# GpSimd's stores become operations of the scheduler, with a price and places of their own

## The chip, the cores and the metric

The kernel runs on one NeuronCore of a Trainium2 chip. The metric is the device time of one execution in microseconds (us). Three runs of the kernel before gave 804.59, 804.32 and 807.07 us; their median is 804.59 us.

Engine names as the profile has them: PE is TensorE (matrix products), PEld its weight loads, DVE is VectorE, ACT is ScalarE, POOL is GpSimd, and SP is SyncE, which here only issues DMAs. An entry such as SPq or POOLq is the queue of DMA issues of that engine.

## The reference, cut to what matters

```python
def _A_ref(x, dft_seq_re, dft_seq_im, dft_hid_re, dft_hid_im):
    a = jnp.einsum("bsd,ed->bse", x, dft_hid_re)
    b = jnp.einsum("bsd,ed->bse", x, dft_hid_im)
    return jnp.einsum("ts,bse->bte", dft_seq_re, a) - jnp.einsum("ts,bse->bte", dft_seq_im, b)

def _B_ref(x, w_gate, w_up, w_down):
    g = jnp.einsum("bsd,df->bsf", x, w_gate)
    u = jnp.einsum("bsd,df->bsf", x, w_up)
    return jnp.einsum("bsf,fd->bsd", _gelu(g) * u, w_down)

xn = _layernorm(x, axis=-1)
return x + _A_ref(xn, ...) + _B_ref(xn, ...)
```

Here x is 1 x 2048 x 512, the sequence matrices are 2048 x 2048, the hidden ones 512 x 512, and the inner width of the gated part is 1792. All is float32. The change touches only how the first part, A, is put in order.

## The kernel before

**Products.** Each float32 operand is split into a high and a low part (ScalarE writes the high part at L241, VectorE the low part at L246), and a product is three matrix products on these parts. On top of that, most products use a scheme of seven block products in place of eight, so an r from 0 to 6 stands in many names.

**Stages.** Part A first multiplies with the sequence matrices: for each of four column blocks c of 512, panels of the matrices are loaded (tiles `pan`), added and subtracted on VectorE (L623, L624), split (`psh`, `psl`), and multiplied into the banks `m`. A step is one value k of this loop. In the first half of a block (p = 0) it loads three panels, makes four operands and runs 24 matrix products; one of its sums is also parked in DRAM (`t2_park`), for the second half (p = 1), which loads two panels and the parked one. After block 1 and block 3 the result is multiplied with the hidden matrices into the banks `y` (seven products r, in the order 0, 1 ahead of block 1 and 4, 2, 6, 5, 3 behind it). ScalarE copies each `y` bank to a tile `part`, and GpSimd stores that tile into the DRAM tensor `partial`. For r = 0, 5, 6 the store is plain; for r = 1, 2, 3, 4 it adds to what lies there (L544 and L546). Part B, the gated part, follows from about 387 us on and is not touched.

**Memory.** All working tiles come from one pool of 109 slots. A tile gets the slot of an older tile, and its first writer waits until the last reader of the older one is done. If that reader is a store, the writer waits until the store has landed.

**What sets the order.** From the start to the first steps of block 2, the order of every engine's instructions comes from a list scheduler, the class `Plan` (L31 to L208). Each operation has an engine, a cost in us, operations that it needs, tiles that it makes and uses, and sometimes a due date. `deadlines` works the other due dates out backwards from the products of TensorE. `run` then plays the program on a model of the five engines: at each turn `choose` takes, per engine, the operation that can start first, or one with an earlier due date that can start nearly as soon, and of these the one that starts first of all. The code of the operations is then emitted in that order, and so each engine's queue has it. The model has one DMA system, `self.dma`, which takes 2.6 us for a megabyte (L179), and a list of what is in flight (`flying`); SP may have eight loads in flight.

GpSimd's DMAs were entered in the model but not ordered by it: the store was issued inside another operation. The copy of `y` on ScalarE issued it (`y_out`, in the operation `yo`), the sum on VectorE issued the parked panel (`sum_step`) and the difference `xd` (`sub_xd`). An operation of GpSimd beside it (`yd`, `park`, `xdp`) did nothing but hold the model's GpSimd and DMA time:

```python
plan.add(("yo", r), "a", 1.04, lambda r=r: y_out(0, r), ...)
plan.add(("yd", r), "g", 1.2, lambda: None, after=[("yo", r)], uses=[("po", r)], mb=2 * MB)
```

From block 2 on, the order is written out by hand in loops; these call the same functions.

**Waits between engines.** SP's loads and GpSimd's stores each go through eight counters in rotation (DMAHW0 to 7, DMASW0 to 7). An issue waits until the DMA eight places before it has landed, since it uses the same counter; so a GpSimd row with `waits DMASW4` also raises DMASW4 itself.

Of the kernel before, what the change touches and what calls it, by code (L numbers as in the profile page):

```python
# [15 lines left out]
S = 2048  # L16
# [19 lines left out]
class Plan:  # L36
# [16 lines left out]
    def add(self, name, engine, cost, fn, after=(), makes=(), uses=(), due=None, mb=0, banks=(), holds=()):  # L53
# [5 lines left out]
        self.ops[name] = dict(e=engine, cost=cost, fn=fn, after=after, makes=dict(makes), due=due, mb=mb, banks=tuple(banks), drains=bool(holds) and engine != "p")  # L59
# [82 lines left out]
    def run(self):  # L142
# [25 lines left out]
        while any(ready.values()):  # L168
# [39 lines left out]
def fnet_geglu_kernel(ctx: ExitStack, tc: tile.TileContext, x, xt, cs, dh, wgu, wd, out):  # L208
# [300 lines left out]
    yps, zraw, zt = {}, {}, {}  # L509
# [14 lines left out]
    def sub_xd(sp, j):  # L524
        nc.vector.tensor_sub(xd[sp, j, 0], xd[sp, j, 0], xd[sp, j, 1])
        nc.gpsimd.dma_start(partial[sp, 2, j], xd[sp, j, 0])
# [11 lines left out]

    def y_out(sp, r, js=range(2)):
        for j in js:  # L540
            t = slot("part")
            nc.scalar.activation(t, yps[r, j], AF.Copy)  # L542
            if r in (0, 5, 6):
                nc.gpsimd.dma_start(partial[sp, r, j], t)  # L544
            else:
                nc.gpsimd.dma_start(partial[sp, r, j], t, accum_op=OP.add)  # L546
# [67 lines left out]
    def sum_step(i):  # L614
# [4 lines left out]
        if p == 0:  # L619
# [4 lines left out]
                    lambda: (nc.vector.tensor_sub(b22, b22, t1), nc.gpsimd.dma_start(t2_park[c, k], b22))]  # L624
# [610 lines left out]
    plan.flying["s"] = [4.4, 5.7, 7., 8.1]  # L1235
    for t in range(2, X_AHEAD):
        plan.done(("x", XO[t]), land)
        plan.flying["s"].append(land)
        land += .675
    for i in range(3, LOAD_AHEAD):  # L1240
        plan.done(("pan", i), land)
        plan.flying["s"].append(land)
# [145 lines left out]
    def step_ops(i, late=None):  # L1388
# [3 lines left out]
        def s(j):  # L1392
            if not box:
                box.extend(sum_step(i))
            box[j]()
        for key in (*PANELS[p], *(["t2"] if p else [])):
            plan.add(("ld", i, key), "s", .45, lambda key=key: load_one(i, key), makes={("r", i, key): 1}, mb=MB, due=late,
                     after=[("S", i - (HS - FIRST[c]), 2)] if key == "t2" else [])
        if p == 0:
# [5 lines left out]
            plan.add(("park", i), "g", .01, lambda: None, after=[("S", i, 2)], mb=MB, uses=[("r", i, b22)])  # L1405
# [169 lines left out]
    for r, g in ((0, 0), (0, 1), (1, 0), (1, 1)):  # L1575
# [3 lines left out]
        if g:  # L1579
            plan.add(("yo", r), "a", 1.04, lambda r=r: y_out(0, r), after=[("y", r, g), *([("res", 0, 0)] if r else ["st2"])],  # L1580
# [168 lines left out]
```

## Time and profile before

| what | before |
|---|---|
| median of three runs | 804.59 us |
| the profiled execution's own time | 804.45 us |
| its span, first to last instruction | 802.4 us |
| PE busy | 794.4 us (99%) |
| DVE busy | 718.8 us (90%) |
| ACT busy | 504.9 us (63%) |
| POOL busy | 156.4 us (19%) |
| granted clock of TensorE, mean over the core | 1.000 |
| stages on PE, from the chain of work that ended last: plain products / block 0 / y / block 1 | from 5.54 / 60.69 / 89.25 / 100.29 us |
| y again / block 2 / y / block 3 / y | from 176.28 / 205.12 / 283.77 / 294.65 / 370.81 us |

The 2.05 us between span and time lie around the span. PE's busy time holds for matrix products only. Times within the trace are us from the start of the span; a row of the timeline has start, duration, engine, line, operation, output tile and input tile, and in brackets how long the engine was idle before it and what ended that. `x2` means that rows of the same kind that follow each other are put together.

### The profile page before, as it was taken

The numbers are of one execution on the slowest core, as the hardware profiler recorded it, in microseconds if no ns is written. First come the engines' busy times: TensorE is split into PE (matmuls) and PEld (weight loads), VectorE is DVE, ScalarE is ACT, GpSimd is POOL, SyncE is SP. The second block draws the span as 40 slices with busy tenths as digits, with TensorE's granted clock in tenths as the row PEclk, the third lists the DMA queues.
The fourth block names the chain that finished last, engine by engine and source line by source line (L and its number), as shares of the span: only waits on it lengthen the run. The fifth ranks groups of instructions, "written<-read, shape, count | busy, mean of one in ns | idle before, by whom it ended". The sixth has DMA issues, their size and how long they took to land.

```text
span 802.4 us, 11459 instructions
## 1 busy us (share of the span) xinstructions
PE 794.4 (99%) x3493; PEld 654.4 (82%) x3493; DVE 718.8 (90%) x1330; ACT 504.9 (63%) x950; POOL 156.4 (19%) x227
## 2 busy tenths in 40 slices
PE   9999999999899999999999999999999999999998
PEld 6888888888688888888888888888888888888886
DVE  7999999969899979899999998898778779989787
ACT  6786566547444465364758776766766677576564
POOL 0001410034211131000203423321221233121100
PEclk9999999999999999999999999999999999999999
DMA  9737797868999988778825987868965799887842
GB/s 333 283 119 259 268 353 256 281 230 233 349 351 315 350 289 296 256 272 268 203 79 128 218 161 172 189 109 217 255 126 96 128 232 153 174 211 137 250 105 105
DMA packets 90110, 176.69 MB, mean 220 GB/s; under 512 B 10784, under 2 KB 14400, under 8 KB 89856
## 3 DMA queue, kind: packets, MB, share of 16 engines
q1 hardware_dynamic: 65040, 117.75, 43.7%
q0 software_dynamic: 24720, 57.95, 33.7%
q8 instruction: 27, 0.44, 0.2%
q14 instruction: 35, 0.29, 0.1%
q10 hardware_dynamic: 288, 0.26, 0.1%
HBM read 113.77 MB, written 65.29 MB: 223 GB/s over the span
## 4 chain that ended last, share of the span: by engine, by line
PE 97%; DMA 1%; DVE 1%; ACT 0%; issue 0%; SPq 0%; DVEq 0%; ACTq 0%
PE m L257 31%; PE dn L257 17%; PE b L257 14%; PE c L257 10%; PE a L257 9%; PE y L257 8%; PE z L257 7%; DMA pan<-in_cs 1%; PE warm L1191 1%; DVE psl L246 0%; ACT part L542 0%; DVE dl L246 0%; DVE zr L1514 0%; DVE z410l L246 0%; ACT dh L241 0%
## 5 line engine op out<-in xcount | busy, mean ns | idle before, releaser
L241 ACT ACTIVATE psh<-pan 128x512 fp32r<-128x512 f32 x189 | 108.7, 626 | 82.1 <-DVE pan L628 30.0
L246 DVE TENSOR_TENSOR psl<-pan,psh 128x512 fp32r<-128x512 f32 x189 | 121.3, 682 | 6.0 <-ACT psh L241 5.3
L907 POOL DMA_DIRECT2D partial<-part x94 | 80.9, 870 | 234.0 <-ACT part L906 200.7
L257 PE MATMUL m<-psl,xch 128*128 128x512 f32 x216 | 84.2, 390 | 0.1
L257 PE MATMUL m<-psh,xch 128*128 128x512 f32 x216 | 84.1, 390 | 0.0
L257 PE MATMUL m<-psh,xcl 128*128 128x512 f32 x216 | 84.1, 389 | 0.0
L906 ACT ACTIVATE part<-dn 128x512 f32<-128x512 f32 x94 | 55.4, 604 | 24.2 <-PE dn L257 22.4
L246 DVE TENSOR_TENSOR wl<-ws,wh 128x512 fp32r<-128x512 f32 x84 | 55.1, 684 | 0.1
L241 ACT ACTIVATE wh<-ws 128x512 fp32r<-128x512 f32 x84 | 49.7, 629 | 0.1
L257 PEld LDWEIGHTS m<-psl,xch 128*128 128x128 f32 x216 | 40.6, 188 | 9.1 <-DVE psl L246 0.6
L257 PEld LDWEIGHTS m<-psh,xch 128*128 128x128 f32 x216 | 40.6, 188 | 8.3
L257 PEld LDWEIGHTS m<-psh,xcl 128*128 128x128 f32 x216 | 40.6, 188 | 8.3
L1131 ACT ACTIVATE w<-b 128x512 f32<-128x512 f32 x28 | 16.7, 598 | 47.1 <-PE b L257 47.0
L624 POOL DMA_DIRECT2D t_park<-pan x27 | 15.1, 558 | 140.3 <-DVE pan L624 90.6
L1134 DVE TENSOR_TENSOR w<-c,w 128x512 f32<-128x512 f32 x28 | 19.3, 689 | 24.6 <-ACT w L1131 24.6
L246 DVE TENSOR_TENSOR htl<-s,hth 128x512 fp32r<-128x512 f32 x56 | 36.0, 686 | 4.5 <-ACT hth L241 4.4
L879 DVE TENSOR_TENSOR s<-s 128x512 f32<-128x512 f32 x56 | 37.4, 688 | 1.0
L257 PE MATMUL m<-psh,xa 128*128 128x512 f32 x108 | 37.7, 389 | 0.0
L623 DVE TENSOR_TENSOR pan<-pan 128x512 f32<-128x512 f32 x54 | 35.3, 678 | 0.0
L246 DVE TENSOR_TENSOR wl<-wx,wh 128x512 fp32r<-128x512 f32 x28 | 19.2, 686 | 16.3 <-ACT wh L241 16.3
L241 ACT ACTIVATE hth<-s 128x512 fp32r<-128x512 f32 x56 | 32.4, 642 | 1.0 <-DVE s L879 1.0
L241 ACT ACTIVATE hh<-s 128x512 fp32r<-128x512 f32 x42 | 26.7, 635 | 9.8 <-DVE s L866 7.3
(779 smaller groups left out, 2379.2 us busy)
## 6 DMA issues: line engine op xcount, KB each, us to landing
pan<-in_cs SPq DMA_DIRECT2D x155, 256.0 KB, 5.4
partial<-part POOLq DMA_DIRECT2D x122, 256.0 KB, 5.1
wx<-in_wgu SPq DMA_DIRECT2D x56, 256.0 KB, 4.9
wd<-in_wd SPq DMA_DIRECT2D x28, 256.0 KB, 4.3
acc<-partial SPq DMA_DIRECT2D x28, 256.0 KB, 5.6
t_park<-pan POOLq DMA_DIRECT2D x27, 256.0 KB, 4.8
pan<-t_park SPq DMA_DIRECT2D x27, 256.0 KB, 4.4
zr<-z_park SPq DMA_DIRECT2D x16, 256.0 KB, 4.9
```

The lines of the kernel that those rows point to most:

```text
L241: nc.scalar.activation(t[0], src, AF.Copy, scale=float(sign))
L246: engine.tensor_sub(t[1], src, hi)
L257: nc.tensor.matmul(ps, a[u][:, sl], b[v], start=first and r == 0, stop=last and r == 2, skip_group_check=resumed)
L623: return [lambda: nc.vector.tensor_sub(t3, b22, b12), lambda: nc.vector.tensor_sub(t1, b12, b11), lambda: (nc.vector.tensor_sub(b22, b22, ...
L624: lambda: (nc.vector.tensor_sub(b22, b22, t1), nc.gpsimd.dma_start(t2_park[c, k], b22))]
L879: nc.vector.tensor_sub(t, u, v)
L906: nc.scalar.activation(t, ps[j], AF.Copy)
L907: nc.gpsimd.dma_start(partial[sp, r, j], t, accum_op=OP.add)
L1131: nc.scalar.activation(w, b, AF.Copy)
L1134: nc.vector.tensor_add(w, c, w)
L1191: nc.tensor.matmul(ps, warm[:, :P], warm, start=i == 0, stop=False)
```

## The change

The change makes each of GpSimd's stores in the scheduled part an operation with code of its own, so that `Plan` sets its place in GpSimd's queue by start time and due date as for other engines. `y_out` is split into `y_copy` (ScalarE) and `y_send` (GpSimd); the hand-written part still calls `y_out`, which does both. The parked panels and `xd` go the same way, and the load of a parked panel now needs the park operation rather than the sum. The model is changed in two points: a store that adds takes 3.3 times the DMA time of a plain one of its size, and GpSimd may have seven DMAs in flight, of which one that adds takes two places. The late due date of the last five copies (`END + 54.4`) goes, so that they fall due 4 us after their product.

```diff
-    def add(self, name, engine, cost, fn, after=(), makes=(), uses=(), due=None, mb=0, banks=(), holds=()):
+    def add(self, name, engine, cost, fn, after=(), makes=(), uses=(), due=None, mb=0, banks=(), holds=(), adds=False):
...
+    def parts(self, o):
+        return round(o["mb"] / .262) * (2 if o["adds"] else 1)
...
                 if e == "s":
-                    at = max([at, o["due"] - self.ahead] + self.flying[e][-8:][:1] * (len(self.flying[e]) > 7))
+                    at = max(at, o["due"] - self.ahead)
+                if o["mb"]:
+                    k, room = self.parts(o), 8 if e == "s" else 7
+                    for when, u in reversed(self.flying[e]):
+                        k += u
+                        if k > room:
+                            at = max(at, when)
+                            break
...
-                self.dma = max(self.dma, at + o["cost"] + 1.1) + o["mb"] * 2.6
+                self.dma = max(self.dma, at + o["cost"] + 1.1) + o["mb"] * 2.6 * (3.3 if o["adds"] else 1)
                 end = self.dma + self.LAND
-                self.flying[e].append(end)
+                self.flying[e].append((end, self.parts(o)))
...
+    def y_copy(r, js=range(2)):
+        for j in js:
+            ypart[r, j] = slot("part")
+            nc.scalar.activation(ypart[r, j], yps[r, j], AF.Copy)
+
+    def y_send(sp, r, js=range(2)):
+        for j in js:
+            nc.gpsimd.dma_start(partial[sp, r, j], ypart.pop((r, j)), **({} if r in (0, 5, 6) else {"accum_op": OP.add}))
...
-            plan.add(("park", i), "g", .01, lambda: None, after=[("S", i, 2)], mb=MB, uses=[("r", i, b22)])
+            plan.add(("park", i), "g", .6, lambda: nc.gpsimd.dma_start(t2_park[c, k], pan_src[i][5]), after=[("S", i, 2)], mb=MB, uses=[("r", i, b22)])
...
-        plan.add(("yo", r), "a", 1.04, lambda r=r: y_out(0, r), after=[("y", r, 1), *OUT.get(r, ())], makes={("po", r): 2}, holds=both,
-                 due=END + 54.4)
-        plan.add(("yd", r), "g", 1.2, lambda: None, after=[("yo", r)], uses=[("po", r)], mb=2 * MB)
+        plan.add(("yo", r), "a", 1.04, lambda r=r: y_copy(r), after=[("y", r, 1), *OUT.get(r, ())], makes={("po", r): 2}, holds=both)
+        plan.add(("yd", r), "g", 1.2, lambda r=r: y_send(0, r), after=[("yo", r)], uses=[("po", r)], mb=2 * MB, adds=r in (1, 2, 3, 4))
```

**How the order moves.** TensorE's order is the same instruction for instruction. On the other engines few rows change place, nearly all in the `y` stage behind block 1; many more tiles get another slot, and with it other waits.

ScalarE in that stage, before (`z…h` and `dh` are high parts of operands, `part<-y` the copies of two banks of one r: r = 4, then 2):

```order
L241 ACTIVATE z210h<-m_1361 128x512
L241 ACTIVATE z211h<-m_1369 128x512
L241 ACTIVATE dh<-ds 128x512 x2
L241 ACTIVATE z600h<-zt 128x512
L241 ACTIVATE z601h<-zt 128x512
L241 ACTIVATE dh<-ds 128x512 x2
L241 ACTIVATE dh<-d 128x512
L542 ACTIVATE part<-y 128x512 x2
```

And now:

```order
L251 ACTIVATE z210h<-m_1361 128x512
L251 ACTIVATE z211h<-m_1369 128x512
L251 ACTIVATE dh<-ds 128x512
L553 ACTIVATE part<-y 128x512 x2
L251 ACTIVATE z601h<-zt 128x512
L251 ACTIVATE z500h<-zr 128x512
L251 ACTIVATE dh<-ds 128x512 x2
L251 ACTIVATE dh<-d 128x512
```

The copies of r = 4 moved ahead of `z601h` and of three `dh`; in GpSimd's queue their two adding stores moved ahead of one pair of `d_park` stores in the same way.

VectorE at the end of that stage and at the first step of block 2, with each instruction's waits, before (`z311l` is the last low part of the `y` stage; `pan<-pan` are the sums of a step, `psl` its low parts):

```order
L246 TENSOR_TENSOR z310l<-zr,z310h 128x512 [waits PE_49,Activation_49]
L246 TENSOR_TENSOR z311l<-zr,z311h 128x512 [waits DMASW4_49,Activation_49]
L623 TENSOR_TENSOR pan<-pan 128x512 [waits DMAHW6_49,DMAHW5_49]
L623 TENSOR_TENSOR pan<-pan 128x512 [waits DMAHW4_49,PE_49]
L624 TENSOR_TENSOR pan<-pan 128x512 [waits DVE_49]
```

And now, to the sums of the second step:

```order
L256 TENSOR_TENSOR z311l<-zr,z311h 128x512 [waits PE_49,Activation_49]
L639 TENSOR_TENSOR pan<-pan 128x512 [waits DMAHW5_49,DMAHW6_49,DMASW2_49,PE_49]
L639 TENSOR_TENSOR pan<-pan 128x512 [waits DMAHW4_49,PE_49]
L640 TENSOR_TENSOR pan<-pan 128x512 [waits DVE_49]
L256 TENSOR_TENSOR psl<-pan,psh 128x512 [waits DMASW1_49,PE_49,Activation_49]
L256 TENSOR_TENSOR psl<-pan,psh 128x512 [waits Activation_49]
L256 TENSOR_TENSOR psl<-pan,psh 128x512 [waits PE_49,Activation_49]
L256 TENSOR_TENSOR psl<-pan,psh 128x512 [waits DMASW3_49,Activation_49]
L639 TENSOR_TENSOR pan<-pan 128x512 [waits DMAHW1_49,DMAHW0_49]
L639 TENSOR_TENSOR pan<-pan 128x512 [waits DMAHW7_49,DMASW7_49,DMASW5_49]
```

`z311l` now gets a slot that a matrix product gave up, where it had that of a `part` tile under an adding store (DMASW4, the second one of r = 2). The next tile on VectorE that waits for a store of `part` is one of the second step (DMASW7, the first store of r = 6); the counters DMASW1 to 3 in between stand for `d_park` stores.

SP's queue some rows on, the loads around the fourth to sixth step, before:

```order
L522 DMA xd<-in_xt 128x512 [waits DMAHW4_49,DMASW5_49]
L736 DMA bst<-mean_rstd 128x512 [waits DMAHW5_49,DVE_49]
L736 DMA bst<-mean_rstd 128x512 [waits DMAHW6_49,DMASW4_49,PE_49]
L740 DMA xr<-in_xt 128x512 [waits DMAHW7_49,DMASW1_49]
L609 DMA pan<-in_cs 128x512 [waits DMAHW0_49,DMASW4_49]
```

And now:

```order
L532 DMA xd<-in_xt 128x512 [waits DMAHW4_49,DMASW2_49]
L752 DMA bst<-mean_rstd 128x512 [waits DMASW5_49,DMAHW5_49,DMASW4_49,Activation_49]
L752 DMA bst<-mean_rstd 128x512 [waits DMAHW6_49,DVE_49]
L756 DMA xr<-in_xt 128x512 [waits DMAHW7_49,DMASW1_49,PE_49]
L625 DMA pan<-in_cs 128x512 [waits DMAHW0_49]
```

The wait for the second store of r = 5 (DMASW4) sat on the first panel of the sixth step; it now sits on the first `bst` load, three rows ahead of that panel.

More of the change, by code (lines that the diff above doesn't have):

```diff
@@ L58, in add @@
             self.products = name
-        self.ops[name] = dict(e=engine, cost=cost, fn=fn, after=after, makes=dict(makes), due=due, mb=mb, banks=tuple(banks), drains=bool(holds) and engine != "p")
+        self.ops[name] = dict(e=engine, cost=cost, fn=fn, after=after, makes=dict(makes), due=due, mb=mb, adds=adds, banks=tuple(banks), drains=bool(holds) and engine != "p")
         self.size.update(makes)
@@ L537, in y_block @@
                         part=part, late=1)
+    def y_copy(r, js=range(2)):
[5 more added lines that the diff above has]
+            nc.gpsimd.dma_start(partial[sp, r, j], ypart.pop((r, j)), **({} if r in (0, 5, 6) else {"accum_op": OP.add}))
     def y_out(sp, r, js=range(2)):
         for j in js:
[L541 to L546, printed above, removed]
+            y_copy(r, [j])
+            y_send(sp, r, [j])
     def fetch_z(sp, kb, g):
@@ L1234, in fnet_geglu_kernel @@
     plan.dma, land = 12.8, 8.75
[L1235 removed]
+    plan.flying["s"] = [(t, 1) for t in (4.4, 5.7, 7., 8.1)]
     for t in range(2, X_AHEAD):
         plan.done(("x", XO[t]), land)
[L1238 removed]
+        plan.flying["s"].append((land, 1))
         land += .675
```

25 lines of the change are left out of this document (13 added, 12 removed).

## The prediction

> **What bounds the kernel now.** I read the page's head first, then the waits of PE, then PE's timeline where these waits fall.
>
> ```profile
> span 802.4 us, 11459 instructions
> PE 794.4 (99%) x3493; PEld 654.4 (82%) x3493; DVE 718.8 (90%) x1330; ACT 504.9 (63%) x950; POOL 156.4 (19%) x227
> ```
> ```profile
> PE m L257 <- DVE psl L246: 1.6, 1, 1.6
> PE warm L1191 <- DVE eps L1188: 1.2, 1, 1.2
> PE y L257 <- DVE z311l L246: 0.9, 1, 0.9
> ```
> ```profile
> 100.29 72.77 PE m L257 x321
> ```
>
> PE is busy in 99% of the span, and waits three times in the whole program. TensorE's order does not change, so a change of order elsewhere can only win what PE loses now. PE's cadence is 72.77 / 321 = 0.2267 us per product (the row of the chain of waits: start, length, what, how many). Two of the three waits (columns: total, times, longest) lie at the passage from the `y` stage to block 2:
>
> ```profile
> 181.68 0.61 PE L257 MATMUL y<-z411l,dh 128*128 128x512 f32 x2
> ...
> 202.99 0.61 PE L257 MATMUL y<-z310l,dh 128*128 128x512 f32 x2
> 204.54 0.73 PE L257 MATMUL y<-z311l,dh 128*128 128x512 f32 x2 [0.94 <-DVE z311l L246]
> ...
> 207.08 0.50 PE L257 MATMUL m<-psl,xa 128*128 128x512 f32 x1 [1.57 <-DVE psl L246]
> ...
> 209.45 0.39 PE L257 MATMUL m<-psh,xch 128*128 128x512 f32 x1
> ```
>
> From 202.99 to 209.45 PE starts 13 products. These need 13 x 0.2267 = 2.95 us and took 6.46, so **3.5 us** are lost here (the two bracketed waits, 2.5, and about a microsecond in smaller pieces that the waits do not list). VectorE over the same stretch:
>
> ```profile
> 198.20 0.69 DVE L246 TENSOR_TENSOR z310l<-zr,z310h 128x512 fp32r<-128x512 f32 x1
> 203.80 0.69 DVE L246 TENSOR_TENSOR z311l<-zr,z311h 128x512 fp32r<-128x512 f32 x1 [4.91 <-DMA partial<-part]
> 204.41 1.28 DVE L623 TENSOR_TENSOR pan<-pan 128x512 f32<-128x512 f32 x2
> ```
>
> `z311l` stands 4.91 us for a store of `part`; the sums of block 2's first step queue behind it, and their `psl` comes late for PE. One wait on VectorE makes both waits of PE. GpSimd shows which store it is:
>
> ```profile
> 187.21 1.81 POOL L546 DMA_DIRECT2D partial<-part  x2 [3.00 <-ACT part L542]
> 188.41 1.18 POOL L410 DMA_DIRECT2D d_park<-dh  x1
> 189.01 1.12 POOL L410 DMA_DIRECT2D d_park<-dl  x1
> 194.03 0.89 POOL L546 DMA_DIRECT2D partial<-part  x1 [3.90 <-ACT part L542]
> 196.74 0.87 POOL L546 DMA_DIRECT2D partial<-part  x1 [1.81 <-ACT z310h L241]
> ```
> ```profile
> partial<-part POOLq DMA_DIRECT2D x1, 256.0 KB, 7.0
> ```
>
> The last line is the group of issues around 196.74: landing 7.0 us later, at 203.7, where `z311l` starts. The bracket at 194.03 names ScalarE's copies, but those were done at 189.8 (next fence), 4.2 us before. The two adds of r = 4 and two plain stores make 2 x 2 + 2 = 6 of seven places, so an add (two places) cannot go until the first add has landed: 187.21 plus the 6.5 us of that issue is 193.7, and the next add issues at 194.03. The trace so agrees with the change's count of places.
>
> **The change, part by part.** *`z311l` gets another slot.* It now waits for PE and ScalarE alone, and no longer for a store. VectorE, free at 198.20 + 0.6 = 198.8 rather than 203.8, is 5.0 us earlier. PE's need for it is at 202.99 + 2 x 0.2267 = 203.4; it is ready at 199.5. PE reaches its first product of block 2 at 203.90 and needs the first `psl` at 204.1. The panels of that step were issued from 185.09 on and landed in a median of 4.5 us:
>
> ```profile
> pan<-in_cs SPq DMA_DIRECT2D x7, 256.0 KB, 4.5
> ...
> d_park<-dh POOLq DMA_DIRECT2D x1, 256.0 KB, 9.0
> ```
>
> The three that the step needs were the first of these seven and are there by 193.7 even at 8 us. The sums take 2.0 and the first `psl` 0.69, so from 199.5 on VectorE has it ready at about 202.2. Gain: 3.5 us.
>
> *The copies of r = 4 go ahead of three `dh` and of `z601h` on ScalarE.*
>
> ```profile
> 181.90 0.63 ACT L241 ACTIVATE dh<-ds 128x512 fp32r<-128x512 f32 x1 [3.16 <-DVE ds L429]
> ...
> 183.96 0.63 ACT L241 ACTIVATE z601h<-zt 128x512 fp32r<-128x512 f32 x1 [0.90 <-DVE zt L1523]
> ...
> 186.20 1.06 ACT L542 ACTIVATE part<-y 128x512 f32<-128x512 f32 x2
> ...
> 188.72 1.08 ACT L542 ACTIVATE part<-y 128x512 f32<-128x512 f32 x2
> ```
>
> PE finished r = 4 at 182.3 (row 181.68 above), so they can run from 182.5, and their adds issue near 183.1, about 4 us earlier. Those of r = 2 can then go out at 189.8 to 193.5 instead of 194.03 and 196.74. The 1.06 us of copying now stands ahead of the four other rows; ScalarE idles 0.9 us within them and PE shows no wait on any of them. Price: nothing on the path. If that cover were gone, it would cost at most 1.06.
>
> *The next wait for a store of `part` on VectorE.* It is at the second step's second sum, ten operations behind `z311l` (first store of r = 6).
>
> ```profile
> 198.45 0.82 POOL L544 DMA_DIRECT2D partial<-part  x1
> ...
> 204.56 0.54 POOL L544 DMA_DIRECT2D partial<-part  x1
> 205.30 0.54 POOL L544 DMA_DIRECT2D partial<-part  x1 [0.20 <-issue]
> ```
> ```profile
> partial<-part POOLq DMA_DIRECT2D x1, 256.0 KB, 8.5
> ```
>
> The store of 198.45 took 8.5 us and landed at 206.95. VectorE reaches that sum at about 198.8 + 9 x 0.6 = 204.2: it waits between 0 (the queue runs earlier now) and 2.75 us. Behind it stand the rest of the sums and the step's `psl`, ready at 206.95 + 1.2 + 0.69 = 208.8. PE needs the first of them 24 products after 203.90, at 209.3 plus one cadence, 209.6. Price: 0 up to 206.95 + 0.8; from there a microsecond for a microsecond.
>
> *SP's queue: `bst`, `bst`, `xr` ahead of the sixth step's panels.* The wait for r = 5's second store now stands three rows earlier.
>
> ```profile
> 212.48 1.82 SPq L609 DMA_DIRECT2D pan<-in_cs  x3
> ```
> ```profile
> partial<-part POOLq DMA_DIRECT2D x2, 256.0 KB, 7.1
> ```
> ```profile
> pan<-in_cs SPq DMA_DIRECT2D x1, 256.0 KB, 9.5
> ```
> ```profile
> 226.61 1.28 DVE L623 TENSOR_TENSOR pan<-pan 128x512 f32<-128x512 f32 x2
> ```
>
> The stores of 204.56 and 205.30 land 7.1 us later, the second at 212.4; there SP went on with the panels. Three issues now come first, at the 1.82 / 3 = 0.61 of the row +1.8; the last of the panels went out at 212.48 + 2 x 0.61 = 213.7, landing 9.5 later at 223.2, and so comes in at 225.0. VectorE's sums at 226.61 move up by its 5.0 to 221.6, so it can stand up to 3.4 us. The sums take 2.0, two `psl` 1.3, so these are ready at 228.3. PE needs it 5 steps after 203.90, 203.90 + 5 x 24 x 0.2267 = 231.1. Price: 0, by 2.8 us.
>
> *What VectorE keeps of the 5.0.* PE gains 3.5 where VectorE gains between 1.6 (after those 3.4) and 5.0. At the turn to r = 3's part in block 2 PE waits for a short chain, VectorE's L690 and ScalarE's L691, whose result PE reads about 248.8 by the new time (203.90 + 8.25 steps of 5.44):
>
> ```profile
> 250.10 1.20 ACT L691 ACTIVATE m<-u 128x512 f32<-128x512 f32 x2 [2.42 <-DVE u L690]
> ```
>
> The first copy ends near 250.7; minus 1.6 that is 249.1, minus 5.0 it is 245.7. Price: 0 to 0.3, and 0.9 if VectorE kept only 1.0 of its lead. I take **0.3**: the small lead follows from SP's rows, the large one only from nothing else being late.
>
> *Rows that cost nothing.* In block 0's `y` stage and in the fetch of `zr` some loads and parked panels swap places; PE shows no wait in either stage, and VectorE's only waits between 178 and 300 us are these two:
>
> ```profile
> DVE psl L246 <- ACT psh L241: 5.0, 5, 4.4
> DVE z311l L246 <- DMA partial<-part: 4.9, 1, 4.9
> ```
>
> No operation is added or removed; the bytes are the same. From block 2's middle on the text is the old one.
>
> **Sum:** 804.45 - 3.5 + 0.3 = **801.3 us**. The profiled execution lies 0.14 below the median 804.59, which is nothing here. That is 0.4% less, while about 0.5%, 4.0 us, is what a measurement of this kernel can tell from no change: the forecast is a gain too small to be called one.
>
> The stores moved forward move into a stage that the loads share (columns: stretch; length; PE, PEld, DVE, ACT, POOL busy and instructions; clock; DMA share; GB/s):
>
> ```profile
> 176.00:187.00 11.00, 10.87 (x48) 8.69 (x48) 10.81 (x19) 6.33 (x13) 2.16 (x4) 1.00 0.37 131
> 187.00:199.00 12.00, 12.00 (x55) 9.94 (x54) 11.89 (x20) 8.85 (x17) 6.08 (x9) 1.00 1.05 274
> ...
> 210.00:250.00 40.00, 40.00 (x178) 33.10 (x177) 39.05 (x65) 17.47 (x32) 6.86 (x12) 1.00 1.01 342
> ```
>
> The engines of the DMA are a third busy to 187 and full after it. The adds of r = 4 move into the empty part, which relieves the full one. The Trainium skill, DMA: Bandwidth & Descriptors, section "Issuing engines are not separate DMA queues", says that DMAs from any engine run on the same 16 DMA engines and interleave, which speaks against the change: what GpSimd wins in its queue, SP's loads lose. The share of 1.05, with loads and stores in it, agrees. By that rule, with DMA full from 187, the stores that come earlier push SP's panels back by their own time. The sum would then be that of the first rival below.
>
> **Rivals.**
>
> *1. The stall moves to the second step's panels.* In the new order SP's ninth and eleventh panel load of the fetch wait for the two adds of r = 2. The second of these landed at 203.7. If the adds come, in a DMA that is full, only 2 us earlier, the eleventh load goes out at 201.7 and lands 7.5 us later (between the 6.5 and 8.5 of the stores), at 209.2; 1.2 + 0.69 later, at 211.1, the step's first `psl` is ready, against PE's 209.6: 1.5 us of the 3.5 are lost again. Time: about 803; with no lead at all and 8.5 us it is 4.5 us and 805.8. For it: a DMA share of 1.05. Against it: by ScalarE's rows the adds go out up to 4 us earlier.
>
> *2. The change does not remove the wait, or puts one as long at the same place.* If another tile of that step (the first sum, or `psl`) stands for a store that lands at 207 to 208, `psl` is ready near 208 to 209 as now. Time: 804.4. For it: several first-step tiles now wait for `d_park` stores, whose landings took up to 9 us. Against it: these were issued by 189.01 and landed by 198 (188.41 + 9.0 = 197.4, its partner behind it).
>
> *3. Slower: SP stands behind r = 5's second store.* Every load from the fourth step's `bst` on waits for it. The landing can be late by 2.8 us (212.4 to 215.2) without price; from there each microsecond is one of PE. To pass 808.6 it must give back the 3.2 and cost 4.1 more, a landing at 222.5, 17.2 us after the issue at 205.30; the slowest store shown took 9.0. For it: DMA share 1.01 to 250 us and VectorE busy 39.05 of 40, so nothing is caught up. Against it: that store is not issued later by any row.
>
> **How the numbers follow.** Forecast (between 800.9 and 802.0 by itself: all 3.5 without a price, to 1.0 of price) 0.62; rival 1 0.18, of it 0.05 past 804.6; rival 2 0.07; rival 3 0.08, of it 0.05 past 808.6; a gain over 4.0, to 800.5 or less, 0.05: this needs the 3.5 and half a microsecond more from places where the waits show nothing. Of the forecast, 0.05 lies under 800.6 once the scatter of two medians is taken in (the three runs spread over 2.8 us). So faster 0.10, same 0.85, slower 0.05. The range 800.3 to 804.6 leaves out the end of rival 1, rival 3 and part of the gain beyond.
>
> **What would show it.** Right: `z311l` starts near 198.8 with no bracket; PE's `y` and `m` rows are 0.23 apart from 202.99 to 209; PE's list of waits keeps `warm` alone; the adds of r = 4 issue near 183 and those of r = 2 by 193.5. Wrong: a bracket of a store on VectorE's L639 beyond 207.7, panels of the fetch landing beyond 207.7 (rival 1), SP's L752 released beyond 215 (rival 3), or a new wait of PE on `m` near 249 larger than 1.0.

## The result

The changed kernel takes **800.47 us** (median of 5 runs, 800.13 to 801.47) where the kernel before took 804.59 (5 runs, 804.32 to 807.07). The medians differ by 4.1 us. The ratio is 0.9941, with a 95% interval of 0.9923 to 0.9958: faster, by 0.6%. (It is close to the ratio of the means, 805.38 and 800.59; two of the five runs of the kernel before are long, 807.07 and 806.33.) The forecast was 801.3 us and a gain too small to be called one. The time lies in the stated range and 0.8 us below the forecast; that the gain could not be told from no change was wrong.

| | before | after |
|---|---|---|
| median of the runs | 804.59 us | 800.47 us |
| the profiled execution's own time, and its span | 804.45, 802.4 us | 800.63, 798.7 us |
| block 2 on PE begins | 205.12 us | 204.05 us |
| `y` behind block 2 begins | 283.77 us | 280.37 us |
| part B begins | 387.13 us | 383.73 us |
| the last stretch of part B begins | 779.20 us | 775.50 us |

Of the 3.7 us of span, 3.40 are won by the end of block 2; they are carried through unchanged to part B, where 0.30 more come. The changed kernel's PE waits (total, times, longest) over the whole program:

```profile
PE warm L1207 <- DVE eps L1204: 1.2, 1, 1.2
PE y L267 <- DVE dl L256: 0.2, 1, 0.2
```

Both waits at the passage are gone; the 0.2 is a new one ahead of it, at 179.6 us. PE's timeline there, and VectorE's:

```profile
203.14 0.61 PE L267 MATMUL y<-z310l,dh 128*128 128x512 f32 x2
203.59 0.62 PE L267 MATMUL y<-z311l,dh 128*128 128x512 f32 x2
204.05 0.39 PE L267 MATMUL m<-psh,xa 128*128 128x512 f32 x1
204.28 0.39 PE L267 MATMUL m<-psl,xa 128*128 128x512 f32 x1
...
206.09 0.39 PE L267 MATMUL m<-psh,xch 128*128 128x512 f32 x1
```
```profile
198.85 0.69 DVE L256 TENSOR_TENSOR z310l<-zr,z310h 128x512 fp32r<-128x512 f32 x1
199.45 0.68 DVE L256 TENSOR_TENSOR z311l<-zr,z311h 128x512 fp32r<-128x512 f32 x1
200.06 1.29 DVE L639 TENSOR_TENSOR pan<-pan 128x512 f32<-128x512 f32 x2
```

The 13 products that took 6.46 us up to `m<-psh,xch` now take 206.09 - 203.14 = 2.95, the cadence itself. `z311l` has no bracket and ends some 3.5 us ahead of PE. GpSimd around the stores:

```profile
184.29 1.81 POOL L557 DMA_DIRECT2D partial<-part  x2 [3.76 <-ACT part L553]
185.49 1.18 POOL L420 DMA_DIRECT2D d_park<-dh  x1
186.09 1.14 POOL L420 DMA_DIRECT2D d_park<-dl  x1
187.74 0.56 POOL L420 DMA_DIRECT2D d_park<-dh  x1 [0.51 <-ACT dh L251]
189.11 0.54 POOL L420 DMA_DIRECT2D d_park<-dl  x1 [0.82 <-DVE dl L256]
192.06 1.83 POOL L557 DMA_DIRECT2D partial<-part  x2 [2.41 <-ACT z501h L251]
```

The adds of r = 4 go out at 184.29 (187.21 before), those of r = 2 from 192.06 (194.03 and 196.74 before).

### The profile page after: what moved, and what is told of

Same layout as the page of the kernel before. It is cut to its first block, busy times and chain, and to the rows that moved or that the text cites. A ratio compares the mean times of both kernels' runs of the same rounds, so it can differ in the third digit from the quotient of the medians.

```text
span 798.7 us, 11467 instructions
## 1 busy us (share of the span) xinstructions
PE 793.4 (99%) x3493; PEld 654.4 (82%) x3493; DVE 718.9 (90%) x1330; ACT 504.5 (63%) x950; POOL 156.7 (20%) x227
## 4 chain that ended last, share of the span: by engine, by line
PE 99%; DVE 1%; issue 0%; ACT 0%
PE m L267 32%; PE dn L267 17%; PE b L267 14%; PE c L267 10%; PE a L267 10%; PE y L267 9%; PE z L267 7%; PE warm L1207 1%; DVE zr L1530 0%; DVE zt L1539 0%; DVE dl L256 0%; ACT z200h L251 0%; DVE ds L433 0%; DVE z410l L256 0%; DVE p L1002 0%
## 5 line engine op out<-in xcount | busy, mean ns | idle before, releaser
L923 POOL DMA_DIRECT2D partial<-part x94 | 81.0, 872 | 234.1 <-ACT part L922 208.8
L557 POOL DMA_DIRECT2D partial<-part x28 | 20.8, 777 | 114.5 <-ACT part L553 108.7
L267 PE MATMUL dn<-hl,wh 128*128 128x512 f32 x84 | 32.8, 390 | 0.0
```

Of the source, the lines that this page charges most:

```text
L267: nc.tensor.matmul(ps, a[u][:, sl], b[v], start=first and r == 0, stop=last and r == 2, skip_group_check=resumed)
L557: nc.gpsimd.dma_start(partial[sp, r, j], ypart.pop((r, j)), **({} if r in (0, 5, 6) else {"accum_op": OP.add}))
```

## The experiments

The theory from the prediction ("slot"): what counts is whose slot `z311l` got, and when the last reader of that slot lands. The rivals: the earlier stores themselves bring the gain, or the price, the places or the due date does. Each time is a median, with its range. The experiments ran on three chips, each with the kernel before timed beside it on the same chip.

### Which part of the change brings it

**a1.** The changed kernel once more, unedited.

> The changed kernel once more, for a second profile and a second set of times. If the 0.30 us that it won in part B (PE's row c: 1.63 us before, 1.39 after) belongs to the change, PE's part B again takes 396.9 us less its end's shift as in the first profile, and the time is 800.1 to 801.0. If it is scatter, the entry into part B stays at 383.7 us and the rest varies by 0.1 to 0.4.

Measured: 800.12 us (799.85 to 800.73, 6 runs). Its part B took 775.05 - 383.24 = 391.81 us between the two marks of the table; the first profile gives 391.77, the kernel before 392.07 (392.07 or 392.08 in its three later profiles too). So the 0.30 comes with the change. Most of it is one weight load of `c`, which waits for VectorE; in the kernel before, then in the changed one:

```profile
398.01 0.19 PEld L257 LDWEIGHTS c<-xT20h,wh 128*128 128x128 f32 x1 [0.40 <-DVE w L1134]
```
```profile
394.34 0.19 PEld L267 LDWEIGHTS c<-xT20h,wh 128*128 128x128 f32 x1 [0.16 <-DVE w L1150]
```

**a2.** The kernel before, with two slots of their own for the `part` tiles of r = 2:

```diff
-    mem = ctx.enter_context(tc.tile_pool(name="mem", bufs=SLOTS))
+    mem = ctx.enter_context(tc.tile_pool(name="mem", bufs=SLOTS - 2))
+    own = ctx.enter_context(tc.tile_pool(name="own", bufs=2))
...
-            t = slot("part")
+            t = own.tile([P, D], F32, name="part", tag="own") if (sp, r) == (0, 2) else slot("part")
```

> The kernel before with its order on every engine; only the two part tiles of r = 2 lie in a pool of their own (two slots, and two fewer in the common pool), so that z311l cannot get their slot and waits for PE and ScalarE alone. The adding stores go out as late as before (194.0 and 196.7). Theory (the slot is the cause): PE's passage into block 2 has no gap, 804.5 - 3.4 = 801.1, 800.5 to 801.7. Rival (the stores must go out earlier, since something else of these steps waits for them or for DMA): the gap stays at 2 us or more, 803 to 804.5.

Measured: 801.23 us (800.39 to 802.82, 6 runs). GpSimd is as late as before, VectorE no longer waits at `z311l`:

```profile
194.06 0.89 POOL L547 DMA_DIRECT2D partial<-part  x1 [4.20 <-ACT part L543]
196.22 0.87 POOL L547 DMA_DIRECT2D partial<-part  x1 [1.27 <-ACT z301h L242]
```
```profile
198.57 0.69 DVE L247 TENSOR_TENSOR z311l<-zr,z311h 128x512 fp32r<-128x512 f32 x1
...
207.38 1.29 DVE L624 TENSOR_TENSOR pan<-pan 128x512 f32<-128x512 f32 x2 [2.57 <-DMA partial<-part]
```

One slot, and nothing of the change, gives most of the gain (the kernel before beside it: 804.88). The stores of r = 6 are still late here, and the next tile that waits for one stands 2.57 us; PE's waits for `psl` sum to 0.6 in this profile. In the changed kernel r = 6's first store issues at 196.32 (198.45 before) and that wait is gone.

**a3, a4.** The changed kernel with the price alone, and with the places alone:

```diff
a3:
-                    k, room = self.parts(o), 8 if e == "s" else 7
+                    k, room = self.parts(o), 8 if e == "s" else 10**6
a4:
-                self.dma = max(self.dma, at + o["cost"] + 1.1) + o["mb"] * 2.6 * (3.3 if o["adds"] else 1)
+                self.dma = max(self.dma, at + o["cost"] + 1.1) + o["mb"] * 2.6 * (1 if o["adds"] else 1)
```

> The changed kernel with the price of 3.3 for an adding store, but without the count of places on GpSimd's queue in the model (room without limit). z311l waits for PE and ScalarE alone. Theory (slot): as the changed kernel, 800.5, within 0.5. Rival (the count of places brings the gain): 1 us or more above it.

> The changed kernel with the count of places, but an adding store at the price of a plain one. GpSimd's order up to block 2 is that of the changed kernel, but z311l has the slot of r = 2's second adding store again. That store landed at 201.6 in the changed kernel (issued 193.0, 8.6 later). Theory (slot, and the landing of its last reader): z311l starts at 201.7, the first psl is ready at 201.7 + 0.6 + 2.0 + 0.69 = 205.0, PE needs it at 204.3: 0.5 to 1.0 lost, 801.0 to 801.5. Rival 1 (any wait for a store there costs the whole 3.4): 803.5 to 804. Rival 2 (early stores alone bring the gain, the slot is indifferent): 800.5.

Measured: a3 800.33 us (800.10 to 800.70, 6 runs), a4 801.80 us (801.74 to 802.19, 7 runs). a3 is the changed kernel within 0.2. In a4 GpSimd's order at these stores is the changed kernel's, only `z311l` sits under r = 2's second add again:

```profile
201.72 0.69 DVE L256 TENSOR_TENSOR z311l<-zr,z311h 128x512 fp32r<-128x512 f32 x1 [2.15 <-DMA partial<-part]
```

It starts at 201.72, as worked out from the landing. PE's listed waits for `psl` are 0.7; the time is 1.6 above the changed kernel's where 0.5 to 1.0 were expected. In its profile the 13 products take 4.22 us (203.15 to 207.37), 1.27 above the cadence, so PE again loses more there than its waits list; and part B takes 392.05, 0.28 more than in the changed kernel. That VectorE waits for a store is thus worth 1.6 or 3.4 us by when the store lands, and both of a4's rivals (the whole 3.4, or nothing) fall.

**b2, b3, b4.** The kernel before without the late due date; the changed kernel with the due date put back; the stores as operations and nothing else (no price, no places, the due date kept):

```diff
b2 (on the kernel before):
-        plan.add(("yo", r), "a", 1.04, lambda r=r: y_out(0, r), after=[("y", r, 1), *OUT.get(r, ())], makes={("po", r): 2}, holds=both,
-                 due=END + 54.4)
+        plan.add(("yo", r), "a", 1.04, lambda r=r: y_out(0, r), after=[("y", r, 1), *OUT.get(r, ())], makes={("po", r): 2}, holds=both)
b3 (on the changed kernel; b4 has a3's and a4's edits too):
-        plan.add(("yo", r), "a", 1.04, lambda r=r: y_copy(r), after=[("y", r, 1), *OUT.get(r, ())], makes={("po", r): 2}, holds=both)
+        plan.add(("yo", r), "a", 1.04, lambda r=r: y_copy(r), after=[("y", r, 1), *OUT.get(r, ())], makes={("po", r): 2}, holds=both,
+                 due=END + 54.4)
```

> The kernel before with one edit: the late due date of the last five copies of y goes. The copies of r = 4 move ahead of the dh as in the changed kernel, and z311l gets the slot of a d_park store issued near 189, z310l that of r = 2's first adding store. Theory (slot and landing): the first lands by 198, the second by about 200.2 if the adds run as in the changed kernel, so z310l starts at 200.2 instead of 198.8 and the first psl is ready at 200.3 + 1.2 + 2.0 + 0.69 = 204.2 against PE's 204.2: loss 0 to 0.5, 800.6 to 801.3. Rival (the stores must be operations of their own): no gain, 803.5 to 804.6.

> The changed kernel with the late due date of the last five copies put back: the copies and the adds of r = 4 and r = 2 go out about as late as in the kernel before. z311l gets the slot of r = 4's first adding store, issued near 187, landing by 196. Theory (slot and landing): no wait at z311l, no gap, 800.2 to 801.2. Rival (the earlier copies and adds bring the gain): 803 to 804.5.

> The stores as operations of their own and nothing else of the change: no price, no count of places, the late due date kept. z311l gets the slot of r = 4's second adding store, and the first step's first psl that of r = 2's second one, whose landing was 203.7 before. Theory (slot and landing): z311l does not wait, psl starts at 203.7 and is ready at 204.4 against PE's 204.3: 0.1 to 0.7 lost, 800.7 to 801.5. Rival (price and places bring the gain): 803 to 804.5.

Measured: b2 801.13 us (800.79 to 801.27, 5 runs), b3 800.84 (800.68 to 801.08, 5 runs), b4 802.17 (801.82 to 802.64, 11 runs). Every one of them beats the kernel before beside it (805.00) by 2.8 us or more. Where VectorE still waits for a store, it is at the tile that the new slots say (b2, then b4; b4 has a further wait of 0.95 at a sum of the first step, which was not expected):

```profile
200.32 0.69 DVE L246 TENSOR_TENSOR z310l<-zr,z310h 128x512 fp32r<-128x512 f32 x1 [1.99 <-DMA partial<-part]
```
```profile
204.29 2.50 DVE L256 TENSOR_TENSOR psl<-pan,psh 128x512 fp32r<-128x512 f32 x4 [1.63 <-DMA partial<-part]
```

b4 is above its expected range, by a term that was not in it: with the due date kept, PE waits for ScalarE's late copy of a bank `y`. From b4's list (b3's has 1.0):

```profile
PE y L267 <- ACT part L553: 1.1, 1, 1.1
```

So no single part of the change carries the gain. The kernel before had an unlucky slot: `Plan` counts how many slots are free, not which one a tile gets, and four of the five other orders tried (a3, b2, b3, b4) give `z311l` another one. That the change gives it a harmless one is in this sense luck. The price and the earlier due date add what remains: with both (a3 and the changed kernel), no wait at the passage.

**c3.** The kernel before, with the stores of r = 4 and r = 2 plain (the sum is left out there):

```diff
-            if r in (0, 5, 6):
+            if r in (0, 5, 6) or (sp, r) in ((0, 4), (0, 2)):
```

> The kernel before, with the stores of r = 4 and r = 2 in the scheduled part stored plain and not added (the sum in partial is left out there; bytes and order stay). Theory (an adding store takes two of seven places on GpSimd): with one place each, the stores of r = 2 issue at 189.8 to 191 instead of 194.0 and 196.7, land by 200, z311l waits 1 us or less, no loss on PE: 800.5 to 801.5. Rival (what holds them is the order or a full DMA, not the kind of store): they issue near 194 and 196.7 again, 804 to 805.

Measured: 800.78 us (800.31 to 800.96, 6 runs). GpSimd:

```profile
186.88 1.17 POOL L544 DMA_DIRECT2D partial<-part  x2 [2.98 <-ACT part L542]
188.03 0.55 POOL L410 DMA_DIRECT2D d_park<-dh  x1
188.63 0.54 POOL L410 DMA_DIRECT2D d_park<-dl  x1
189.41 1.14 POOL L544 DMA_DIRECT2D partial<-part  x2 [0.24 <-issue]
190.54 0.54 POOL L410 DMA_DIRECT2D d_park<-dh  x1
192.96 0.54 POOL L410 DMA_DIRECT2D d_park<-dl  x1 [1.88 <-DMA partial<-part]
```

Plain stores of the same bytes in the same order go seven deep without a wait for a landing. The eighth goes out at 192.96, 0.3 us after the first of them has landed (186.88 + 5.8). With adds it was four (two adds, two plain) and then a wait. "Two of seven" holds here. `z311l` starts at 198.65 without a wait.

### Where the other microsecond comes from

The kernel before was timed 110 times in all beside these runs and as b1. Each run has a mean granted clock of TensorE (the clock that the chip let it have, as a share of full speed), and the times go with it:

| mean granted clock | runs of before | median, range | runs of the changed kernel |
|---|---|---|---|
| 0.999 to 1.000 | 47 | 803.67 us, 801.55 to 805.37 | all 11, median 800.23 us |
| 0.997 to 0.998 | 44 | 805.33 us, 804.22 to 806.95 | none |
| 0.994 to 0.996 | 19 | 806.99 us, 806.43 to 807.86 | none |

At full clock the two differ by 803.67 - 800.23 = 3.4 us, the gap. Over all runs (median 804.95) they differ by 4.7.

**b1, c4, d4.** The kernel before, unedited: b1 was timed, c4 and d4 are one profiled execution each. In the expectations, theory A is that a pause of PE lowers the clock, theory B that the landing of the store makes the spread (in e1: that the low clock has another cause), and theory C that something else that comes with a late `z311l` lowers the clock.

> The kernel before once more, for a second profile. The three runs shown spread over 2.8 us, those of the changed kernel over 1.3. If the landing of the store under z311l sets the passage, a later landing makes a longer run: PE's loss between 202.99 and 209.45 was 3.5 in a run of 804.45; a run of 806 to 807 would show 5 to 6 there. If the spread is elsewhere, the loss at the passage is 3.5 again whatever the time.

> The kernel before, one look. 40% of its runs so far have a mean granted clock of 0.995 to 0.998. If this one has, its trace shows in which stretch: theory A says from 205 us on, right behind PE's pause; if it lies elsewhere (in the first 200 us, or in part B far from the pause), the pause is not its cause. With a clock of 1.000 the trace only adds one more loss at the passage, 2.5 to 4 us.

> The kernel before, one look, to catch a run with a lowered clock. Theory A: the low clock lies right behind the pause at 205 to 215 us, and the pauses there are longer than the 1.4 and 1.6 us of the look that kept its clock.

Measured: b1 805.54 us (801.55 to 806.90, 12 runs; its profile is of a run of 804.24 at 1.000, VectorE's wait 4.8), c4 804.64 at 1.000, d4 806.92 at 0.995. PE in d4, and its stretches (start and end; length; busy us of PE, PEld, DVE, ACT, POOL; granted clock; DMA share; GB/s):

```profile
202.36 0.61 PE L257 MATMUL y<-z310l,dh 128*128 128x512 f32 x2
204.71 0.73 PE L257 MATMUL y<-z311l,dh 128*128 128x512 f32 x2 [1.73 <-DVE z311l L246]
205.28 0.40 PE L257 MATMUL m<-psh,xa 128*128 128x512 f32 x1
207.24 0.79 PE L257 MATMUL m<-psl,xa 128*128 128x512 f32 x1 [1.57 <-DVE psl L246]
...
212.10 0.63 PE L257 MATMUL m<-psh,xch 128*128 128x512 f32 x1
212.53 0.63 PE L257 MATMUL m<-psl,xch 128*128 128x512 f32 x1
212.96 0.50 PE L257 MATMUL m<-psh,xcl 128*128 128x512 f32 x1
213.30 0.40 PE L257 MATMUL m<-psh,xch 128*128 128x512 f32 x1
```
```profile
205.00:210.00 5.00, 3.43 (x10) 2.37 (x10) 4.96 (x9) 3.69 (x7) 2.25 (x4) 0.64 1.04 410
210.00:215.00 5.00, 5.00 (x17) 3.99 (x16) 5.00 (x10) 2.11 (x4) 1.43 (x2) 0.68 1.04 327
215.00:220.00 5.00, 5.00 (x24) 4.14 (x23) 4.81 (x9) 2.50 (x5) 0.56 (x1) 1.00 1.07 310
```

Behind the two pauses the products start 0.43 us apart (212.10 to 212.53) and take 0.63 where 0.39 is usual, until 213: about half speed. The clock is 1.00 again from 215 on. PE loses a second time behind its wait.

**c1, c2, d2, d3.** The changed kernel with `z311l` computed 1 + n times over, for n = 8, 20, 6, 7: a delay with no DMA in it, planned as 0.60 us for each repeat. (In the code, 1 + n stands for the numbers 9, 21, 7 and 8.)

```diff
-        plan.add(("zlo", key), "v", V5, lambda: split_lo(z[key], src()), after=[("zhi", key)], uses=[*uses, ("z", key)], **kw)
+        plan.add(("zlo", key), "v", V5, lambda: [split_lo(z[key], src()) for _ in range(n + 1 if key == (3, 1, 1) else 1)], after=[("zhi", key)], uses=[*uses, ("z", key)], **kw)
```

> The changed kernel, with z311l computed nine times over on VectorE (the same values), 8 x 0.60 = 4.8 us of delay that no DMA can shift. z311l is ready at 200.1 + 4.8 = 204.9 against PE's need at 203.6, and the first psl at 202.7 + 4.8 = 207.5 against 204.3: PE loses 3.2 to 3.5, as in the kernel before, and 800.4 becomes 803.7 at a clock of 1.000. Theory A (a pause of PE of this length is itself what now and then lowers the granted clock, and the spread of the kernel before is that): runs at a clock of 0.995 to 0.998 appear here too, up to 807. Theory B (the spread comes from the landing of the store): all runs within 803.2 to 804.2 and clocks of 0.999 to 1.000.

> The same with 20 extra computations, 12.0 us: PE loses 10.4 to 10.7, and VectorE has that much less lead behind. At a clock of 1.000 the time is 811 to 812. Theory A: low clocks at least as often as in c1. Theory B: clocks of 0.999 to 1.000, and 811 to 812 in all runs.

> z311l 6 x 0.60 = 3.6 us late. PE waits 0.1 to 1.1 for it and 1.6 to 2.0 for psl, 2.2 in all: 802.4 to 802.9 without a lower clock, 804.5 to 805.3 with one as in c1 (2.4 more). Theory A with a limit near 3 us: no low clock. If half of the runs have it, the limit lies lower.

> z311l 7 x 0.60 = 4.2 us late. PE loses 2.8 to 3.2, about as in the kernel before: 803.0 to 803.7 without a lower clock, up to 806 with one. Theory A with a limit near 3 us: runs of both kinds, as in the kernel before.

**d1, e1.** The pause filled: c1's kernel with 12, and the kernel before with 6, products of zeros ahead of the one that waits for `z311l`.

```diff
+                if (r, g, e) == (3, 1, 0) and part == slice(2, 3) and not filled:
+                    filled.append(1)
+                    for _ in range(12):
+                        nc.tensor.matmul(yps[r, 1], warm[:, :P], warm, start=False, stop=False)
```

> The kernel of c1 (z311l 4.8 us late), with twelve products of zeros added into a bank of y on PE just ahead of the product that waits for z311l: 12 x 0.22 = 2.6 us of work in place of a pause of 2.3. What VectorE delivers, and when, is as in c1, so the work behind starts as late; only PE does not stand idle there, and a pause of 1.6 for psl remains. Theory A (the pause itself lowers the clock): clocks of 0.999 to 1.000, 803.8 to 804.5, about 2.4 us less than c1 although it computes more. Theory C (something else that comes with the late z311l lowers it, such as full DMA or VectorE's load): 806.4 to 807.2 and 0.995 as in c1.

> The kernel before, with six products of zeros added into a bank of y on PE just ahead of the product that waits for z311l: 6 x 0.22 = 1.3 us of work in the place of the pause there (0.9 to 1.7 in the looks). The store under z311l lands when it did. Theory A (PE's pause lowers the clock, and this spreads the kernel before): clocks of 0.999 to 1.000 in nearly all runs, none at 0.995, 802.0 to 805.0, so that what is left of the spread is the landing of the store. Theory B (the low clock has another cause): 0.995 to 0.998 in 40% of the runs as before, up to 807.

Measured, in the order of PE's pauses at the passage:

| kernel | pauses of PE in the profile, us | runs at a clock of 0.998 or less | median, range, us |
|---|---|---|---|
| changed, with a1 | none | 0 of 11 | 800.23, 799.85 to 801.47 |
| a4 | 0.6 and 0.15 | 0 of 7 | 801.80, 801.74 to 802.19 |
| e1 (before, filled) | 1.0 | 1 of 12 | 802.95, 800.94 to 805.33 |
| d1 (n = 8, filled) | 1.5 | 0 of 11 | 805.28, 804.94 to 805.63 |
| d2 (n = 6) | 0.8 and 1.6 | 4 of 11 | 804.31, 803.59 to 805.86 |
| d3 (n = 7) | 1.5 and 1.6 | 9 of 12 | 806.15, 804.24 to 806.80 |
| before | 0.8 to 1.7, and 1.6 | 63 of 110 | 804.95, 801.55 to 807.86 |
| c1 (n = 8) | 2.3 and 1.6 | 12 of 12 | 806.61, 806.38 to 807.25 |
| c2 (n = 20) | 11.0 and 0.9 | 5 of 5, 0.989 to 0.991 | 815.54, 815.27 to 816.35 |

The share of runs at a low clock goes with the pause. That the pause is its cause is shown by c1 against d1: the same delay on VectorE, 2.4 us more work on PE (203.17 to 205.60), and the low clock goes in all 11 runs; d1 is 1.3 us faster than c1. The two ran on different chips, but the kernel before, timed beside each, has 803.81 and 803.71 at full clock; and on d1's own chip d3, with a shorter delay, has 9 of 12 runs at a low clock and is 0.9 us slower than d1. So theory C falls, and theory B as the cause of the low clock. The row of zeros, then c1's stretch and d1's:

```profile
203.17 2.76 PE L553 MATMUL y<-warm 128*128 128x512 bf16 x12
205.60 0.80 PE L267 MATMUL y<-z311l,dh 128*128 128x512 f32 x2
```
```profile
210.00:215.00 5.00, 5.00 (x17) 3.94 (x16) 4.97 (x9) 2.32 (x4) 2.34 (x3) 0.66 0.99 319
```
```profile
210.00:215.00 5.00, 5.00 (x22) 4.15 (x23) 4.96 (x9) 2.33 (x4) 2.34 (x3) 1.00 1.04 316
```

How long the clock was halved can be read from its column, as 2 x (1 - clock) x length. In d2's profile:

```profile
205.00:210.00 5.00, 3.44 (x10) 2.72 (x10) 4.93 (x9) 3.98 (x8) 0.54 (x1) 0.66 1.04 407
210.00:215.00 5.00, 5.00 (x24) 4.11 (x23) 4.96 (x9) 1.72 (x4) 2.34 (x4) 1.00 1.03 321
```

This gives 3.4 us in d2, 6.8 in d4 (rows above) and in c1, and 17 in c2: one, two, two and five times 3.4. The half clock sets in before the last pause ends (in d2 near 206.3, with the pause until 206.57), and in the 3.4 us ahead of that PE stood idle for 2.1 to 2.4 us in each of the four profiles. In the profiles of a4, e1 and d1 no stretch of 3.4 us holds more than 1.7 us of idle PE (e1's one run at a low clock has no profile); in those of the kernel before and of d3 one can hold 2.4, and they have runs of both kinds. It thus looks as if the idle sum within such a stretch decides; this is read from the profiles and was not tested by itself.

e1 does the same for the kernel before: low clocks in 1 run of 12 where the kernel before beside it, on the same chip, had 12 of 17, and a ratio to it of 0.9977 (0.9961 to 0.9993). What spread it keeps, 800.9 to 804.2 at full clock, is then left to the landing of the store, whose wait on VectorE was 4.8, 4.9, 5.3 and 5.7 us in the four profiles of the kernel before; that part was seen, not isolated.

In d1, d2 and d3 the times without a low clock (medians 805.28, 803.88 and 804.26) are 0.6 to 1.5 us above what was expected, and c2 is 3.5 above; c1 has no run without a low clock. The delays were longer than planned: in c1 the nine computations take from 199.00 to 205.43, against 0.61 for one, so each repeat took 0.73 us and not 0.60. That makes `z311l` 0.7 (d2) to 1.0 us (c1, d1) later, and 2.6 in c2; the smaller losses that the waits do not list, and in c2 the half clock, come on top. One thing stays open: in c1 the runs at 0.998 are no shorter than those at 0.995 (806.62 and 806.59 in the median).

## Why the prediction was right or wrong

**The bound: right.** The loss was 3.5 us at the passage, by one wait of VectorE for the second adding store of r = 2. It went completely: the 13 products take 3.51 us less. At `y` behind block 2 that is 3.4, since the second profile comes to the passage 0.15 later.

**`z311l`'s slot: right.** a2 shows it alone, a4 puts it back. Its start was forecast near 198.8 and is 199.45, because the rows ahead on VectorE came 0.65 later; it cost nothing.

**Copies and adds: right in direction, late by 1 to 2 us.** The copies of r = 4 run at 183.28 (182.5 forecast), the adds issue at 184.29 (183.1), those of r = 2 at 192.06 and 193.01 (189.8 to 193.5). The count of places that the prediction read from one issue holds again here: with r = 4's second add and four plain stores in flight, six of seven, r = 2's first add had to wait.

**The next store of `part`, and SP's queue: priced 0, and 0.** VectorE's waits between 178 and 300 us in the changed kernel name no DMA:

```profile
DVE psl L256 <- ACT psh L251: 4.9, 4, 4.5
DVE p L701 <- PE m L267: 0.3, 1, 0.3
```

In a2, where the order is the old one, the wait at the second step's sum is there (2.57, the forecast's upper end was 2.75), and PE lost 0.6 by it. The second profile of the changed kernel (a1) has one wait for a load, 0.9 us for a panel at 222.9, that PE does not feel. SP's queue came out better than forecast, not 1.8 later but 1.1 earlier, and 0.4 in a1 (the kernel before had its sixth step's panels at 212.48):

```profile
209.78 0.98 SPq L752 DMA_DIRECT2D bst<-mean_rstd  x2
210.87 0.44 SPq L756 DMA_DIRECT2D xr<-in_xt  x1
211.36 1.55 SPq L625 DMA_DIRECT2D pan<-in_cs  x3
```

The forecast had held the landing of r = 5's second store fixed; its issue moved from 205.30 to 203.07.

**The 0.3 at the turn: wrong, it is 0.** It rested on the panels being late, which they were not. VectorE kept 3.7 of its lead, and the copies run at

```profile
246.45 1.28 ACT L707 ACTIVATE m<-u 128x512 f32<-128x512 f32 x2 [2.17 <-DVE u L706]
```

within the forecast's two ends, ahead of PE.

**The step that failed** is the one from the sum to the conclusion: "about 0.5%, 4.0 us, is what a measurement of this kernel can tell from no change". No row gave that figure. Measured, the interval of the ratio reaches 0.18%, 1.4 us, to each side with five runs of each kind, and b4's gain of 0.36% stands clear of no change (0.9952 to 0.9977). The forecast's own gain of 0.4%, 3.3 us, could thus have been told from no change, and so could the 0.6% measured.

The gain was also put too small. Of the 0.8 us between 801.3 and 800.47, 0.3 is the turn that cost nothing, 0.30 came in part B, for which the sum had no term, and 0.16 is the distance of the changed kernel's profiled execution from its median. And the sentence "The profiled execution lies 0.14 below the median 804.59, which is nothing here" hides a loss that the sum has no term for. That execution ran at a clock of 1.000, with no low clock behind its pause. Over many runs, those of the kernel before with the low clock (63 of 110) lie 1.7 or 3.3 us higher in the median, and the changed kernel has none. The sum of the pauses was the gain of that one execution; the price of a pause is its length and, in part of the runs, a stretch at half clock behind it. The three runs shown (804.32 to 807.07) had the clue, a spread of 2.8 us, which the prediction used only to widen its chances.

The Trainium skill, TensorE: Matmul & The Clock Gate, section "Part 1: The HAM clock gate (the "warmup" mystery)", has this rule: the array's clock is halved after an idle window of about 3.4 us and restored after a busy one, and the windows run free of the program. The traces agree with the half clock (0.43 against 0.23 us between products), with the length (3.4, 6.8 and 17 us at half clock) and with chance from run to run. They differ on the limit that the same page draws from it, that gaps of PE above about 3.4 us are to be avoided: here pauses of 0.8 and 1.6 us with three products between them sufficed in 4 of 11 runs. Two pauses near each other seem to count together, while one of 1.5 us never did in 11 runs. The prediction did not see that the rule speaks for this change.

**The rivals.** The first (the stall moves to the second step's panels) did not come: no DMA is in VectorE's list above, and a1's wait of 0.9 cost PE nothing. DMA was as full as it assumed (a share of 1.04 from 187 to 210 us), and this decided nothing. The second (the wait stays, or another of its length takes its place) is what a4, b2 and b4 show in smaller sizes; the change itself escaped it. The third (SP stuck, slower) did not come.

## What to carry to other kernels

A short pause of TensorE can cost more than its length, so a kernel that is 99% busy and has pauses that sum to 2 to 3 us in one place is worth repairing, and the spread of its times and the mean granted clock of each run tell whether it is paying. When the tensor engine waits for an operand that has been computable for long, look at who last read the slot that it is written to: a store's landing binds its slot (here until 5 to 9 us after the issue where the DMA share is 1.0, and 2.3 for the plain stores issued near 180 us, where the share is 0.25), and another slot can do as much as another order. Take the difference from several runs of each kind, not from one profiled execution, and take what can be told from no change from the scatter of such runs.

## What the runs showed of the hardware that was not expected

- PE's products run at about half speed (0.43 us apart, 0.63 us each) behind pauses as short as 0.8 and 1.6 us, in part of the runs. The clock was halved for 3.4 us in d2's profile (mean clock 0.998), 6.8 in d4's and c1's (0.995) and 17 in c2's (0.989), each a multiple of 3.4, and from before the last pause ended.
- Filling a pause with products of zeros keeps the clock: d1 is 1.3 us faster than c1 with 12 products more, and 0.9 faster than d3 on its own chip.
- GpSimd's queue takes seven plain stores of 256 KB before the next one waits (c3); one that adds takes two of these places (in the changed kernel, r = 2's first add waited with one add and four plain stores in flight).
- A repeat of a computation on VectorE into the same tile took 0.73 us, where different tiles follow each other every 0.60 (c1, d2).
